# A prologue with its first x load issued ahead of the diagonal, its masks made by one sum each, and fewer filler matmuls

## The chip, the core and the metric

The kernel runs on one core of one Trainium2 chip. A core has five engines that work side by side, each through its own queue in order: TensorE (PE; PEld are its weight loads), VectorE (DVE), ScalarE (ACT), GpSimd (POOL) and SyncE (SP). SP, ACT and POOL also issue transfers, which 16 DMA engines carry out. The metric is the device time of one execution in microseconds; lower is better.

## The reference: what is computed

A causal convolution over seven tokens, with one set of seven softmax weights per head (8 heads of 24 channels), and then a multiplicative feed-forward layer:

```python
w = np.exp(weight - weight.max(-1, keepdims=True)); w = w / (w.sum(-1, keepdims=True) + 1e-9)
x_pad = np.concatenate([np.zeros((B, 6, 192)), x], axis=1)          # x: 8 x 3904 x 192
out = np.einsum('hk,bskhg->bshg', w, x_pad[:, idx].reshape(B, S, 7, 8, 24))
x = out.reshape(31232, 192)
a, b = x @ w1, x @ w2                                               # 192 x 1024 each
return (a * b @ w3) @ w_out                                         # 1024 x 1024, 1024 x 192
```

## The kernel before, in words

The 31232 tokens are cut into two streams of 15616 (four sequences each), which go through the kernel side by side, and each stream into 31 rounds of up to 512 tokens. `W_sb = w3 @ w_out` is formed once early on. A round is then a first product (`first_product`, L633: the matmuls `pa` with w1 and `pb` with w2; ScalarE copies `pa` to `asb`, L640; VectorE multiplies, L643), and a second product with `W_sb` (`second_product`, L659). 64 channels of both streams share the 128 partitions, so each weight is kept twice, as `wn` and, with its halves exchanged, as `ws` (`swap_w`, L227).

The convolution is itself a matmul. A window of 32 tokens of x (six of them before the 26 tokens that it yields) is multiplied by `Aband`, a 32x32 band matrix per head, present once in each of four groups of 32 partitions. Groups 0 and 2 hold the windows of stream 0 and 1 for the first block. Block 0 has 20 windows per stream; the first six of each are loaded by SP in float32 into `begin` (L193, L197) and cast into the block's tile `xb` (L299), the other fourteen by GpSimd with a cast on the way (`load_x(0)`, L165, one transfer per stream).

Everything that the change touches lies ahead of the first first product, in some 9 us of straight-line code. Its order is written out by hand (a manual schedule: each engine runs its instructions in the order in which the code names them, and waits are derived from the tiles). The prologue goes like this:

- `taps` is loaded, and its softmax formed: `low` (L264), the exponential on ScalarE (L265), the reciprocal (L275), and `share` (L276), which holds the weights on a diagonal over the heads.
- `diag`, a 128x136 tile with ones where the column is the partition, is made on GpSimd by a memset and `affine_select` (L200, L201). From it come `cmask` (four copies, L216) and `every` (four copies through `identities`, L270), four identities of 32x32 side by side on every group of partitions.
- TensorE spreads `share` over the partitions (`spread`, L281), VectorE copies it (`wsb`, L286) and multiplies it into the mask (`cprod`, L292), TensorE gathers that with `every` (`bps`, L305), and VectorE casts the outcome to `Aband` (L309).
- Between these TensorE runs matmuls on a tile of zeros, whose outcome nobody reads: `warm` (L246), and `fill` (L258), which has `Aband` as its operand and so stands behind it in the queue.
- GpSimd, after its two x transfers, issues eight transfers of w1 and w2 (L232 to L238), columns 0 to 384 first and 384 to 1024 second; then it swaps the first 256 columns of `wn[0]`, loads x for blocks 1 and 2, and swaps further columns.
- Then come the convolution of block 0 (`conv(0, ...)`, L345, evicted to `convo`, L355), its transposes on TensorE with a few more fillers (`first_transposes`, L435, L254, copied to `xT`, L440), the last swaps and the first product.

For stream 0 the first window begins six tokens ahead of the tensor, so its first rows in `begin` are cleared and loaded by a transfer of their own. For stream 1 one transfer loads all six windows, with six rows of the preceding sequence in the first, and these are cleared in `xb` after the cast (L301).

Of the kernel before, what the change touches and what calls it, by code (L numbers as in the profile page):

```python
# [9 lines left out]
BF16 = mybir.dt.bfloat16  # L10
AX = mybir.AxisListType
ALU = mybir.AluOpType
# [4 lines left out]
def kernel(  # L17
# [10 lines left out]
    nc = tc.nc  # L28

    B, S, D = x.shape  # L30
    H, K = weight.shape
    G = D // H
    DFF = moe_w1.shape[1]
    JT = DFF // 128
    PAD = K - 1

    NS = 2
    TS = B * S // NS
    CH = 512
# [6 lines left out]
    C = 32  # L46
    ST = C - PAD
# [7 lines left out]
    HW = 6  # L55
# [35 lines left out]
    def tok(i):  # L91
        return wins[i][0]
# [4 lines left out]
    const = ctx.enter_context(tc.tile_pool(name="const", bufs=1))  # L97
# [18 lines left out]
    x_rows = x.rearrange("b s d -> (b s) d")  # L116


    def shape_of(b):
        n = SIZES[b] // 4  # L120
        m = n // (1 if b < 3 else 2)
        return n, m, n // m

    def parts_of(b):
        return [range(4)] if 4 * shape_of(b)[1] * D <= XN else [range(2), range(2, 4)]

    xb_of, zero_rows = {}, {}

    def group(r, e):
        return slice((2 * r + e) * C, (2 * r + e) * C + C)  # L130
# [13 lines left out]
    def x_jobs(b, part):  # L144
        js = parts_of(b)[part]
        n, m, E = shape_of(b)
        tiles, zeros = xb_of.setdefault(b, {}), []

        def alloc():
            xb = work.tile([128, XN], BF16, tag="xb", bufs=5, name="xb")  # L150
            xb = xb[:, 0:len(js) * m * D].rearrange("p (w d) -> p w d", d=D)
            for j in js:
                tiles[j] = (xb, (j - js[0]) * m)
                for e in range(E):
                    for u in range(m):
                        i = FIRST[b] + j * n + u * E + e
                        if tok(i) % S == 0 and i:
                            zeros.extend(
                                (xb, group(r, e).start, tiles[j][1] + u) for r in range(NS))

        def job(first, last, r, e, s, t, w):
            def run():
                if first:
                    alloc()
                nc.gpsimd.dma_start(  # L165
                    out=tiles[js[0]][0][group(r, e), s:s + w, :],
                    in_=bass.AP(tensor=x.tensor, offset=(r * TS + t - PAD) * D,
                                ap=[[D, C], [E * ST * D, w], [1, D]]))
                if last:
                    zero_rows.setdefault(b, []).extend(zeros)  # L170
            return run

        todo = [(r, e, s, t, w) for e in range(E) for s, t, w in runs_of(b, js, e)
                for r in range(NS)]
        return [job(i == 0, i + 1 == len(todo), *a) for i, a in enumerate(todo)]

    def load_x(b):
        for part in range(len(parts_of(b))):
            for f in x_jobs(b, part):
                f()  # L180
# [4 lines left out]
    begin = work.tile([128, HW, D], FP32, tag="abT", bufs=LAG + 1, name="begin")  # L185
    zeros = const.tile([128, 128], BF16)
    nc.vector.memset(zeros, 0.0)
    for r in range(NS):
        p = group(r, 0).start
        if r == 0:  # L190
            nc.vector.memset(begin[p:p + C, 0, :], 0.0)
        w0 = 1 if r == 0 else 0
        nc.sync.dma_start(out=begin[p:p + C, w0:HW, :], in_=bass.AP(  # L193
            tensor=x.tensor, offset=(r * TS + w0 * ST - PAD) * D,
            ap=[[D, C], [ST * D, HW - w0], [1, D]]))
        if r == 0:
            nc.sync.dma_start(out=begin[p + PAD:p + C, 0, :], in_=x_rows[0:ST, :])  # L197

    diag = const.tile([128, 128 + 8], BF16)
    nc.gpsimd.memset(diag, 1.0)  # L200
    nc.gpsimd.affine_select(  # L201
        out=diag, in_=diag, pattern=[[-1, 128 + 8]], compare_op=ALU.is_equal,
        fill=0.0, base=0, channel_multiplier=1)
    ident = diag[:, 0:128]
    load_x(0)

    nc.scalar.preload_act_table(ACT.Exp)
    KP = K + K % 2
# [2 lines left out]
    share = const.tile([H, H, KP], BF16)  # L211
    nc.vector.memset(share, 0.0)
    cmask = const.tile([128, 2, C], BF16)
    for i in range(4):
        d = diag[i * C:i * C + C, i * C + 2 * i:i * C + 2 * i + C]
        nc.vector.tensor_copy(  # L216
            out=cmask[i * C:i * C + C],
            in_=bass.AP(tensor=d.tensor, offset=d.offset, ap=[d.ap[0], [1, 2], [1, C]]))

    wn = [const.tile([128, DFF], BF16, name=f"wn{k}", tag=f"wn{k}") for k in range(3)]  # L220
    wsw = [const.tile([128, DFF], BF16, name=f"ws{k}", tag=f"ws{k}") for k in range(3)]

    W0, W1, W2 = 384, 640, 768

    def swap_w(k, lo, hi, f, halves=(1, 0)):
        for h in halves:
            f(out=wsw[k][Q * h:Q * h + Q, lo:hi], in_=wn[k][Q - Q * h:2 * Q - Q * h, lo:hi])  # L227
# [3 lines left out]
    for cs in (slice(0, W0), slice(W0, DFF)):  # L231
        nc.gpsimd.dma_start(out=wn[0][:, cs], in_=moe_w1[0:128, cs])  # L232
        nc.gpsimd.dma_start(out=wn[2][0:Q, cs], in_=moe_w1[128:192, cs])
        if cs.start:
            nc.gpsimd.dma_start(out=wn[2][Q:128, cs], in_=moe_w2[128:192, cs])
        nc.gpsimd.dma_start(out=wn[1][:, cs], in_=moe_w2[0:128, cs])
        if not cs.start:
            nc.gpsimd.dma_start(out=wn[2][Q:128, cs], in_=moe_w2[128:192, cs])  # L238
# [4 lines left out]
    def warm(n, wd=CH):  # L243
        t = banks("warm")
        for j in range(n):
            nc.tensor.matmul(  # L246
                t[:, j % 2, 0:wd].rearrange("p (a c) -> p a c", c=128), zeros,
                zeros.unsqueeze(1).to_broadcast([128, wd // 128, 128]), start=True, stop=True)
        return t

    def fill(n, out, operand=None):
        for j in range(n):
            if operand is None:
                nc.tensor.matmul(  # L254
                    out.rearrange("p (a c) -> p a c", c=128), zeros,
                    zeros.unsqueeze(1).to_broadcast([128, 2, 128]), start=True, stop=True)
            else:
                nc.tensor.matmul(out, zeros, operand, start=True, stop=True)  # L258

    warm(6)  # L260

    low = const.tile([H, 1], FP32)
    total = const.tile([H, 1], FP32)
    nc.vector.reduce_max(out=low, in_=taps, axis=AX.X, negate=True)  # L264
    nc.scalar.activation(out=taps, in_=taps, func=ACT.Exp, bias=low, accum_out=total)  # L265
    every = const.tile([128, 4, C], BF16)

    def identities(i):
        ps = slice(i * C, i * C + C)
        nc.vector.tensor_copy(out=every[ps],  # L270
                              in_=diag[ps, ps].unsqueeze(1).to_broadcast([C, 4, C]))

    for i in range(3):
        identities(i)
    nc.vector.reciprocal(out=total, in_=total)  # L275
    nc.vector.scalar_tensor_tensor(  # L276
        out=share[:, :, 0:K], in0=taps.unsqueeze(1).to_broadcast([H, H, K]), scalar=total,
        in1=diag[0:H, 0:H].unsqueeze(2).to_broadcast([H, H, K]), op0=ALU.mult, op1=ALU.mult)
    spread = banks("spread")
    for i in range(4):  # L280
        nc.tensor.matmul(  # L281
            spread[i * C:i * C + C, 0, 0:2 * H].rearrange("p (h k) -> p h k", h=H),
            one_rows, share[:, :, 2 * i:2 * i + 2], start=True, stop=True)
    identities(3)
    wsb = const.tile([128, H, 2, 2], BF16)
    nc.vector.tensor_copy(  # L286
        out=wsb, in_=spread[:, 0, 0:2 * H].rearrange("p (h k) -> p h k", h=H)
            .unsqueeze(3).to_broadcast([128, H, 2, 2]))
    warm(2)

    cprod = stage.tile([128, H, 2, C], BF16, tag="cprod", bufs=1, name="cprod")
    nc.vector.tensor_tensor(  # L292
        out=cprod.rearrange("p h k (s two) -> p h k s two", two=2),
# [3 lines left out]
        op=ALU.mult)  # L297
    for r, w0, w1, f in ((0, 0, HW, A), (1, HW // 2, HW, A), (1, 0, HW // 2, V)):
        f(out=xb_of[0][0][0][group(r, 0), w0:w1, :], in_=begin[group(r, 0), w0:w1, :])  # L299
    p = group(1, 0).start  # L300
    nc.vector.memset(xb_of[0][0][0][p:p + PAD, 0, :], 0.0)  # L301
    Aband = const.tile([128, H, C], BF16)
    bps = banks("bps")
    for k in range(2):
# [3 lines left out]
            start=(k == 0), stop=(k == 1))  # L308
    nc.vector.tensor_copy(out=Aband,  # L309
                          in_=bps[:, 0, 0:C * H].rearrange("p (h s) -> p h s", s=C))  # L310
    fill(2, warm(4, 256)[:, 0, 0:2 * CH // 4], Aband.rearrange("p h s -> p (h s)"))


    xT = [const.tile([128, RING], BF16, name=f"xT{k}", tag=f"xT{k}") for k in range(NP)]
# [114 lines left out]
    def first_transposes():  # L429
        n = SIZES[0] // 4  # L430
        convo = convo_of[0]
        for k, f in enumerate((nc.scalar.copy, nc.vector.tensor_copy, nc.vector.tensor_copy)):
            tps = banks_bf16("tps")
            for w in range(n):
                nc.tensor.transpose(  # L435
                    out=tps[:, w, :],
                    in_=convo[:, w, k].rearrange("p r g -> p (r g)"), identity=ident)
            fill(min(k, 1) + 1 if k < 2 else 0,
                 tps[:, 8:16, :].rearrange("p a b -> p (a b)").bitcast(FP32)[:, 0:256])
            f(out=xT[k][:, 0:4 * n * ST].rearrange("p (c w s) -> p c w s", c=4, w=n),  # L440
              in_=tps[:, 0:n, :].rearrange("p w (c s) -> p c w s", c=4)[:, :, :, 0:ST])
# [301 lines left out]
            swap_w(k, c0, c1, P, h)  # L743

    swap_w(0, 0, 256, P)
    first_transposes()
    for k in (2, 1):
        swap_w(k, 0, W0, A, (1,))
# [25 lines left out]
    starts, chain, begun, room, p = {}, {}, set(), 0, -1  # L774
# [224 lines left out]
```

## Time and profile before

| | before |
|---|---|
| median of 3 runs | 510.67 us (510.4 to 510.77) |
| profiled execution, its own time | 510.84 us |
| span of the profiled execution | 509.1 us |
| TensorE busy in the span | 504.4 us (99%) |
| VectorE, ScalarE, GpSimd busy | 446.2, 349.6, 255.9 us |
| first matmul on zeros | at 1.07 us |
| first matmul of the convolution | at 6.52 us |
| first matmul of the first product | at 8.92 us |

The profile is one execution as the hardware profiler saw it. Rows of the timeline have start, duration, engine, line, operation, output and input, and a count; a group's start is its first instruction's. The chain of work that ended last is followed back from the end, at each step to whatever released it; in it, matmuls are counted to their modelled ends, and therefore a piece can begin a little after its instructions' own start. A transfer's time to landing is counted from its issue.

### The profile page before, as it was taken

What the parts mean: (1) busy time and instruction counts of PE and PEld (TensorE: products, weight loads), DVE (VectorE), ACT (ScalarE), POOL (GpSimd) and SP (SyncE); (2) the same over time, 40 slices, a digit from 0 to 9 for tenths busy, and PEclk for the clock granted to TensorE, in tenths of its full rate; (3) what the DMA queues carried; (4) which work ended last, traced back from release to release, by engine and by line L of the source; (5) the groups of instructions that cost most, each with busy time, mean ns of one, the idle gap of its engine ahead of it and who ended that gap; (6) DMA issues with size and microseconds to landing.
All of it is one profiled execution on the core that took longest, in us unless ns stands there. A gap on an engine that the chain in (4) does not pass through costs nothing.

```text
span 509.1 us, 13680 instructions
## 1 busy us (share of the span) xinstructions
PE 504.4 (99%) x5732; PEld 335.9 (66%) x5732; DVE 446.2 (88%) x402; ACT 349.6 (69%) x390; POOL 255.9 (50%) x340
## 2 busy tenths in 40 slices
PE   8999999999999999999999999999999999999997
PEld 4546864595569557845874596569457855965697
DVE  7898769999999799999999998999999999999930
ACT  6786667746779776577567878763876577457752
POOL 9975201332890799499879945992371056000000
PEclk9999999999999999999999999999999999999999
DMA  9999978999969769980998097629302400230025
GB/s 136 160 170 162 166 150 182 149 156 182 175 41 181 136 150 108 227 110 13 100 232 103 12 167 145 117 29 202 83 1 76 155 2 1 93 96 1 1 65 156
DMA packets 161113, 58.46 MB, mean 115 GB/s; under 512 B 116895, under 2 KB 161051, under 8 KB 161051
## 3 DMA queue, kind: packets, MB, share of 16 engines
q1 hardware_dynamic: 86107, 40.12, 37.7%
q0 software_dynamic: 74784, 17.37, 37.3%
q8 instruction: 45, 0.74, 0.6%
q14 instruction: 17, 0.14, 0.1%
q10 hardware_dynamic: 160, 0.10, 0.1%
HBM read 35.02 MB, written 34.85 MB: 137 GB/s over the span
## 4 chain that ended last, share of the span: by engine, by line
PE 99%; ACT 0%; DVE 0%; issue 0%
PE ops L659 32%; PE pa L633 31%; PE pb L633 31%; PE cps L345 1%; PE wps L731 1%; PE warm L246 1%; PE tps L420 0%; PE ops L684 0%; DVE abT L643 0%; PE tps L435 0%; PE cps L375 0%; ACT asb L640 0%; ACT convo L355 0%; PE bps L305 0%; PE warm L258 0%
## 5 line engine op out<-in xcount | busy, mean ns | idle before, releaser
L643 DVE TENSOR_TENSOR abT<-asb,pb 128x1024 bf16<-128x1024 bf16 x240 | 292.7, 1221 | 29.4 <-ACT asb L640 13.4
L640 ACT CAST asb<-pa 128x1024 bf16<-128x1024 f32 x244 | 247.0, 1012 | 64.0 <-PE pa L633 63.8
L633 PEld LDWEIGHTS <-wn 64*128 64x128 bf16 x1488 | 138.5, 94 | 82.1 <-issue 1.6
L633 PEld LDWEIGHTS <-ws 64*128 64x128 bf16 x1488 | 130.1, 94 | 70.8 <-issue 0.9
L659 PE MATMUL ops<-W_sb,abT 128*128 128x192 bf16 x1936 | 163.5, 246 | 0.0
L659 PEld LDWEIGHTS <-abT 128*128 128x128 bf16 x1936 | 158.6, 98 | 6.3 <-issue 6.3
L664 ACT COPY osb<-ops 128x768 f32<-128x768 f32 (+1 forms) x61 | 48.5, 796 | 81.8 <-PE ops L659 80.0
L633 PE MATMUL pb<-xT,wn 64*128 64x512 bf16 x376 | 103.7, 376 | 0.0
L633 PE MATMUL pa<-xT,ws 64*128 64x512 bf16 x376 | 103.5, 376 | 0.0
L633 PE MATMUL pa<-xT,wn 64*128 64x512 bf16 x376 | 103.0, 376 | 0.1
L633 PE MATMUL pb<-xT,ws 64*128 64x512 bf16 x376 | 102.2, 376 | 0.0
L633 PE MATMUL pb<-side,wn 64*128 64x512 bf16 (+1 forms) x368 | 100.4, 369 | 0.0
L633 PE MATMUL pa<-side,ws 64*128 64x512 bf16 (+1 forms) x368 | 99.4, 369 | 0.0
L633 PE MATMUL pa<-side,wn 64*128 64x512 bf16 (+1 forms) x368 | 99.4, 369 | 0.0
L633 PE MATMUL pb<-side,ws 64*128 64x512 bf16 (+1 forms) x368 | 98.1, 369 | 0.0
L538 DVE SCALAR_TENSOR_TENSOR acc<-raw,wC,acc 128x1024 f32<-128x1024 bf16 (+2 forms) x70 | 84.5, 1208 | 2.1
L596 POOL TENSOR_TENSOR acc<-acc,tmp 128x512 f32<-128x512 f32 (+6 forms) x60 | 70.4, 1177 | 4.3
L584 POOL TENSOR_TENSOR tmp<-acc,wC 128x512 f32<-128x512 bf16 x66 | 68.5, 1038 | 3.5
L920 POOL COPY pace<-abT 1x2 bf16<-1x2 bf16 x28 | 4.9, 174 | 110.0 <-DVE abT L643 110.0
L506 POOL DMA_DIRECT2D rows_c<-in_x_dram x58 | 40.7, 710 | 5.7 <-issue 2.9
L165 POOL DMA_DIRECT2D xb<-in_x_dram x50 | 31.9, 647 | 11.2 <-DMA xb<-in_x_dram 5.0
L538 DVE SCALAR_TENSOR_TENSOR acc<-side,wC,acc 128x1024 f32<-128x1024 bf16 (+1 forms) x20 | 24.4, 1218 | 3.9 <-ACT acc L520 3.4
(83 smaller groups left out, 190.6 us busy)
## 6 DMA issues: line engine op xcount, KB each, us to landing
out_dram<-osb SPq DMA_DIRECT2D x54, 384.0 KB
xb<-in_x_dram POOLq DMA_DIRECT2D x16, 240.0 KB, 7.5
out_dram<-osb SPq DMA_DIRECT2D x12, 192.0 KB
rows_c<-in_x_dram POOLq DMA_DIRECT2D x14, 130.0 KB, 6.9
rows_c<-in_x_dram POOLq DMA_DIRECT2D x14, 128.0 KB, 4.6
xb<-in_x_dram POOLq DMA_DIRECT2D x6, 228.0 KB, 7.9
w3b<-in_moe_w_dram POOLq DMA_DIRECT2D x4, 256.0 KB, 5.0
w3b<-in_moe_w_dram POOLq DMA_DIRECT2D x8, 128.0 KB, 4.3
```

The costliest lines, as they stand in the source:

```text
L165: nc.gpsimd.dma_start(out=tiles[js[0]][0][group(r, e), s:s + w, :], in_=bass.AP(tensor=x.tensor, offset=(r * TS + t - PAD) * D, ap=[[D, C] ...
L246: nc.tensor.matmul(t[:, j % 2, 0:wd].rearrange("p (a c) -> p a c", c=128), zeros, zeros.unsqueeze(1).to_broadcast([128, wd // 128, 128]), ...
L345: nc.tensor.matmul(o.rearrange("p (w g) -> p w g", g=wd)[:, :, c - c0:c1 - c0], Aband[group(r, e), h, :], xb[group(r, e), s:s + m, c:c1], ...
L506: nc.gpsimd.dma_start(out=rows_c[lo:t1, k, r * Q:r * Q + Q], in_=x_rows[r * TS + lo:r * TS + t1, k * Q:k * Q + Q])
L538: nc.vector.scalar_tensor_tensor(out=side_of[p][:, k, o:o + t1 - t0] if last else a, in0=raw[:, HALO + lo - t0 - d:HALO + hi - t0 - d], sc ...
L584: nc.gpsimd.tensor_tensor(out=acc if d == 1 else tmp, in0=pool_raw[lane][:, HALO - d:HALO - d + CH], in1=wC[:, k, K - 1 - d:K - d].to_broa ...
L596: nc.gpsimd.tensor_tensor(out=a, in0=a, in1=tmp[:, lo - t0:hi - t0], op=ALU.add)
L633: nc.tensor.matmul(p[:, r, f * N:f * N + N], w_of(i, k, r)[rs, ft * 128:(ft + 1) * 128], operand(R, k, rs), start=(k == 0), stop=(k == NP ...
L640: nc.scalar.copy(out=asb[:, :, 0:per * N], in_=pa[:, :, 0:per * N])
L643: nc.vector.tensor_tensor(out=ab[:, f0, :, 0:N], in0=asb[:, :, 0:N], in1=pb[:, :, 0:N], op=ALU.mult)
L659: nc.tensor.matmul(ops[:, g // 2, (g % 2) * D:(g % 2) * D + D], ab[:, jt, r, g * 128:(g + 1) * 128], W_sb[:, jt, :], start=(jt == 0), stop ...
L664: nc.scalar.copy(out=osb.rearrange("p (a g) d -> p a (g d)", g=2), in_=ops[:, 0:ng // 2, 0:2 * D])
```

## The change

Six edits, all in the prologue:

- `diag`'s memset moves from GpSimd to VectorE, ahead of the clears of `begin`. GpSimd issues stream 0's x transfer first, then makes the diagonal, then issues stream 1's.
- `cmask` and `every` are each made by one `tensor_reduce` over all 128 partitions, which adds up four columns of `diag`, 34 or 32 apart, instead of by four copies on 32 partitions each. `every` is now complete before the reciprocal; its fourth copy used to stand after `spread`.
- Stream 1's first window is treated as stream 0's: its rows in `begin` are cleared first, one transfer loads windows 1 to 5 and another the 26 rows of the first. The clear in `xb` goes.
- The last of the eight weight transfers, columns 384 to 1024 of `wn[1]`, moves behind the swap of `wn[0]`'s first 256 columns, ahead of x for block 1.
- The fillers: six of 512 columns become five and one of 256; two of 512 become one and one of 256; four of 256 become three; two on `Aband` become one.
- Nothing else changes: the convolution, the transposes and all that follows are the same code.

```diff
+    diag = const.tile([128, 128 + 8], BF16)
+    nc.vector.memset(diag, 1.0)
     for r in range(NS):
         p = group(r, 0).start
-        if r == 0:
-            nc.vector.memset(begin[p:p + C, 0, :], 0.0)
-        w0 = 1 if r == 0 else 0
-        nc.sync.dma_start(out=begin[p:p + C, w0:HW, :], in_=bass.AP(
-            tensor=x.tensor, offset=(r * TS + w0 * ST - PAD) * D,
-            ap=[[D, C], [ST * D, HW - w0], [1, D]]))
-        if r == 0:
-            nc.sync.dma_start(out=begin[p + PAD:p + C, 0, :], in_=x_rows[0:ST, :])
-
-    diag = const.tile([128, 128 + 8], BF16)
-    nc.gpsimd.memset(diag, 1.0)
+        nc.vector.memset(begin[p:p + C, 0, :], 0.0)
+        nc.sync.dma_start(out=begin[p:p + C, 1:HW, :], in_=bass.AP(
+            tensor=x.tensor, offset=(r * TS + ST - PAD) * D,
+            ap=[[D, C], [ST * D, HW - 1], [1, D]]))
+        nc.sync.dma_start(out=begin[p + PAD:p + C, 0, :], in_=x_rows[r * TS:r * TS + ST, :])
+
+    first_x = x_jobs(0, 0)
+    first_x[0]()
     nc.gpsimd.affine_select(
         out=diag, in_=diag, pattern=[[-1, 128 + 8]], compare_op=ALU.is_equal,
         fill=0.0, base=0, channel_multiplier=1)
     ident = diag[:, 0:128]
-    load_x(0)
+    for f in first_x[1:]:
+        f()
...
-    for i in range(4):
-        d = diag[i * C:i * C + C, i * C + 2 * i:i * C + 2 * i + C]
-        nc.vector.tensor_copy(
-            out=cmask[i * C:i * C + C],
-            in_=bass.AP(tensor=d.tensor, offset=d.offset, ap=[d.ap[0], [1, 2], [1, C]]))
+    every = const.tile([128, 4, C], BF16)
+
+    def over_groups(out, step, copies):
+        with nc.allow_low_precision("one term of the sum is 1, the others are 0"):
+            nc.vector.tensor_reduce(
+                out=out, in_=bass.AP(tensor=diag.tensor, offset=diag.offset,
+                                     ap=[diag.ap[0], copies, [1, C], [step, 4]]),
+                op=ALU.add, axis=AX.X)
+
+    over_groups(cmask, C + 2, [1, 2])
...
+        if cs.start:
+            break
         nc.gpsimd.dma_start(out=wn[1][:, cs], in_=moe_w2[0:128, cs])
...
-    warm(6)
+    warm(5)
+    warm(1, 256)
...
-    for i in range(3):
-        identities(i)
+    over_groups(every, C, [0, 4])
...
-    identities(3)
...
-    warm(2)
+    warm(1)
+    warm(1, 256)
...
-    p = group(1, 0).start
-    nc.vector.memset(xb_of[0][0][0][p:p + PAD, 0, :], 0.0)
...
-    fill(2, warm(4, 256)[:, 0, 0:2 * CH // 4], Aband.rearrange("p h s -> p (h s)"))
+    fill(1, warm(3, 256)[:, 0, 0:2 * CH // 4], Aband.rearrange("p h s -> p (h s)"))
...
     swap_w(0, 0, 256, P)
+    nc.gpsimd.dma_start(out=wn[1][:, W0:DFF], in_=moe_w2[0:128, W0:DFF])
     first_transposes()
```

More of the change, by code (lines that the diff above doesn't have):

```diff
@@ L265 @@
     nc.scalar.activation(out=taps, in_=taps, func=ACT.Exp, bias=low, accum_out=total)
[L266 to L271, printed above, removed]
-    for i in range(3):
-        identities(i)
+    over_groups(every, C, [0, 4])
     nc.vector.reciprocal(out=total, in_=total)
```

## The prediction

> **What bounds the kernel now.** I read the page first (busy time and the chain that ended last), then the chain in order of time over the first 20 us, because the change touches nothing later than that, then each engine's timeline over that stretch, and last the DMA issues with their times to landing.
>
> ```profile
> PE 99%; ACT 0%; DVE 0%; issue 0%
> ```
>
> TensorE is the bound. Windows of TensorE alone (stretch, length, busy time, instructions, granted clock, DMA share, GB/s) show where the rest lies.
>
> ```profile
> 0.00:10.00 10.00, 8.70 (x112) 1.00 0.91 131
> ...
> 505.00:509.10 4.10, 0.77 (x10) 0.89 0.61 185
> sum 509.10, PE 504.35; mean PE 50.44
> ```
>
> Of 509.10 us, 4.75 are idle: 1.30 in the first 10 us, 3.33 in the tail, which the change leaves alone, and 0.12 in all the rest. So whatever the prologue saves before the first convolution reaches the end of the kernel one for one, provided that weights and x still arrive in time. But "busy" in the prologue includes matmuls on zeros, which are there to fill time. The chain in order of time (start, duration, what) shows it:
>
> ```profile
> 1.07 2.74 PE warm L246 x6
> ...
> 4.94 0.43 PE bps L305 x2
> 5.37 0.85 PE warm L246 x4
> 6.22 0.37 PE warm L258 x2
> 6.59 0.34 PE cps L345 x16
> ...
> 13.82 0.65 PE pb L633 x6
> ```
>
> The first real work that all later work hangs on is the convolution at 6.59. The fillers stand before it in TensorE's own queue, so the chain names them. What would bind without them is read from VectorE:
>
> ```profile
> 2.38 0.15 DVE L264 TENSOR_REDUCE low<-taps 8x1 f32<-8x7 f32 x1
> 2.46 0.78 DVE L270 COPY every<-diag 32x128 bf16<-32x128 bf16 x3
> ...
> 3.45 0.27 DVE L276 SCALAR_TENSOR_TENSOR share<-taps,total,diag 8x56 bf16<-8x56 f32 x1
> ...
> 4.25 0.42 DVE L292 TENSOR_TENSOR cprod<-cmask,wsb 128x512 bf16<-128x512 bf16 x1
> 4.71 0.45 DVE L299 CAST xb<-begin 32x576 bf16<-32x576 f32 x1
> 5.23 0.14 DVE L301 MEMSET xb<- 6x96 uint32 x1
> 5.41 0.42 DVE L309 CAST Aband<-bps 128x256 bf16<-128x256 f32 x1
> ```
>
> Aband is complete at 5.41 + 0.42 = 5.83, yet the convolution starts at 6.59: 0.76 us later, all of it filler. That gap is what there is to win.
>
> **The fillers.** Removed: one half of a 512-column matmul in each of the first two groups, one 256-column matmul from the group of four, and one of the two on Aband: four times 256 columns, and 0.85 / 4 = 0.21 us each by the chain, 0.85 us in all. Not all is gained. Before the spread products, TensorE waits for share (ready 3.45 + 0.27 = 3.72) with six fillers or with five and a half; gain 0. Before bps it then waits for cprod, ready 4.25 + 0.42 = 4.67, with two fillers or with one and a half: gain 0. After bps three fillers end 0.21 earlier, at 6.01, but the single filler on Aband can't start before 5.83 plus a handover of 0.05, and that filler lasts what the first of its kind lasted (shortest, median and longest in ns):
>
> ```profile
> L258 PE MATMUL warm<-Aband,zeros x2: 367/394/421, 6.0 to 6.2; 128*128 128x256 bf16 x2
> ...
> L254 PE MATMUL tps<-zeros x3: 272/272/273, 7.9 to 8.4; 128*128 128x256 bf16 x3
> ```
>
> So the last filler ends at 5.88 + 0.42 = 6.30 instead of 6.59: **0.29 us**. That is the main term. The same rows carry a correction. A matmul of 256 columns lasts 421 ns in the first filler on Aband, 367 in the second, which ends at 6.59, and 272 among the transposes, while the windows above give a granted clock of 1.00. So TensorE became fast at about 6.5, 5.4 us after its first matmul. If that moment stays at 6.5, the first 0.2 us of an earlier convolution run at the slow rate. The cost lies between 0 and (421/272 - 1) x 0.22 (a short matmul's length; the first 16 take 0.34 together) = 0.12; I take 0.04, since most of those 16 end past 6.5. The sum is then 0.29 - 0.04 = 0.25.
>
> **GpSimd: x ahead of the diagonal.**
>
> ```profile
> 0.82 0.21 POOL L200 MEMSET diag<- 128x136 bf16 x1 [0.29 <-POOLq L983]
> 1.11 0.30 POOL L201 TENSOR_SCALAR_AFFINE_SELECT diag<-diag 128x136 bf16<-128x136 bf16 x1
> 1.54 1.48 POOL L165 DMA_DIRECT2D xb<-in_x_dram  x2
> ...
> 7.45 0.84 POOL L227 COPY ws<-wn 64x256 bf16<-64x256 bf16 x2
> ...
> 11.02 3.62 POOL L227 COPY ws<-wn 64x256 bf16<-64x256 bf16 x10
> ```
> ```profile
> xb<-in_x_dram POOLq DMA_DIRECT2D x2, 168.0 KB, 3.8
> wn<-in_moe_w_dram POOLq DMA_DIRECT2D x2, 160.0 KB, 4.7
> ```
>
> The memset of 0.21 goes to VectorE, where it costs no more than those 0.21, ahead of the mask, which can't begin before 2.0 now. Stream 0's issue (1.48 / 2 = 0.74) runs 0.82 to 1.56, the diagonal about 1.64 to 1.94 instead of 1.11 to 1.41, stream 1's issue 2.07 to 2.81, and the weights follow at 2.81, not 1.54 + 1.48 = 3.02: 0.2 earlier. With 3.8 us to landing (the last number of the two DMA rows), stream 1 lands at 5.9 instead of 2.28 + 3.8 = 6.1, stream 0 at 4.6. Both are ahead of 6.30; had the loads not moved at all, 6.1 would still be ahead of it. So the early issue gains nothing by itself, it only keeps the x out of the way of the gain. The weights' 0.2 is worth keeping, as everything that reads them moves up by 0.25.
>
> **One sum each.** The diagonal is 0.5 later, and the mask needs it. Two reductions of 256 and 512 elements per partition replace eight copies (the last one behind the share). Their price isn't in the trace. From below: the fixed 0.15 of the 8x7 reduction, plus (0.45 - 0.15) / 576 = 0.52 ns per element as in the cast of 576: 0.28 + 0.42 = 0.70. From above: share's (0.27 - 0.15) / 56 = 2.1 ns per element: 0.69 + 1.23 = 1.92. I take the Aband cast, nearest in size: (0.42 - 0.15) / 256 = 1.05 ns, so 0.42 + 0.69 = 1.11. The mask then runs 2.0 to 2.42, low 2.4 to 2.5, the identities to 3.2. The exponential waits for its table anyway:
>
> ```profile
> 1.45 1.28 ACT L207 ACT_TABLE_LOAD   x1 [1.45 <-PEq L983]
> 2.74 0.30 ACT L265 ACTIVATE taps<-taps,low 8x7 f32<-8x7 f32 x1
> ```
>
> share still starts near 3.45, so the reductions cost 0, with about 0.05 us to spare: beyond 1.16 us together they delay share, bps, Aband and the convolution one for one.
>
> **Stream 1's first rows.** The clear of 0.14 at 5.23 leaves VectorE, but Aband waited for bps there (4.94 + 0.43 = 5.37), so that gains 0. Added are a clear of begin (a few tenths at most, hidden ahead of the mask) and a fourth transfer on SP's queue:
>
> ```profile
> 1.76 0.33 SPq L193 DMA_DIRECT2D begin<-in_x_dram  x1
> ```
> ```profile
> q1 hardware_dynamic: 421, 0.29, 27.7%
> ...
> q1 hardware_dynamic: 2, 0.00, 0.1%
> ```
>
> The last two rows count the packets of SP's queue in 0 to 4 us and in 4 to 8 us: the load issued at 1.76 had all but two of its packets done by 4.0, so 2.3 us. The new one, issued behind it by 2.25, then lands at 4.55, and the cast at 4.71 needs it: hidden by 0.15, and by 0.4 before Aband is touched (the cast's 0.45 has to end by 5.41). If it took the 3.8 us of GpSimd's x it would land at 6.05.
>
> **wn[1]'s second half behind the swap.** GpSimd is through eight weight loads at 7.45 today, (7.45 - 3.02) / 8 = 0.55 each; with seven, begun 0.2 earlier, at 6.7. Then it waits for the first weights (4.7 at most after 2.81, so 7.5, where it starts today), swaps for 0.8, issues for 0.55 and comes to what is queued behind, the x of block 1 and the ten copies, 0.6 late at most. The moved weights, issued at 7.5 to 8.3, land 3.8 to 4.7 later, at 11.3 to 13.0; their copies are the third and fourth of the ten from 11.02 (0.39 each, ready at 12.6 today). So these are ready between 12.6 and 13.8. TensorE wants them for the group that the chain has at 13.82; its first matmul starts some 0.2 before that (matmuls overlap by the length of a short one), and 0.25 earlier by the change: 13.4. The middle of the bounds, 13.2, is in time, so I take 0; the worst costs 0.4.
>
> **Sum.** 0.29 - 0.04 + 0 + 0 = 0.25 us. The profiled execution took 510.84, 1.74 more than its span and 0.17 above the median; against its own time the sum is 510.59, against the median of 510.67 it is **510.4**.
>
> **The rivals.** *The fast rate comes later (slower).* With fewer fillers TensorE rests before spread, bps and the filler on Aband, for one half filler's time, 0.2 us, twice, and less the third time. If what makes it fast begins anew at a rest, 5.4 us after 3.8 is 9.2. Between the convolution and the first product lie 15 transposes and three fillers, 15 x 128 + 3 x 256 = 2688 columns, 0.21 us per 256 slow and half that fast. A slow stretch costs half its length: from about 7.3 to 9.2 that is 0.95, net 0.95 - 0.25 = +0.7, so 511.4, and 0.5 us for each further us of delay. It decides from 0.5 us of slow transposes on, where the gain is gone. For it: the rows show a rate change that the clock column doesn't. Against: each rest is shorter than one filler (2.74 / 6 = 0.46), together a tenth of the time before 6.3, and no row shows TensorE slowed by a rest. The Trainium skill ("TensorE: Matmul & The Clock Gate", Part 1: The HAM clock gate) says that the array runs at half rate until it was busy for one window of some 3.4 us, and that the windows run free of the kernel. By that rule a spoilt window means a delay of 3.4 us, to 9.9, and an estimated 511.8; a window that still counts as busy means no delay, and the sum stands. The two speeds agree with the trace; how much rest a window forgives no row shows.
>
> *The reductions are dear.* At 1.92 instead of 1.11 the chain is 0.75 late, net +0.5: 511.2. For it: they are strided and nothing of their kind is in the trace; against: of the VectorE rows above only the one of 56 elements gives such a rate.
>
> *A late arrival eats the gain.* Stream 1's first rows at 6.05 put Aband at 6.95 instead of 5.83: net +0.85, 511.5; a landing 0.25 behind 4.95, or moved weights as late as their bound, give just 510.7 to 510.8. Against: the packet counts above.
>
> *The fillers were not the limit*, and x was: then the convolution starts at 6.5 as before, 510.6. Against: the landings of 5.3 and 6.1.
>
> **How the numbers follow.** 0.2% is 1.02 us, about what a measurement of this kernel can tell from no change; the main term is a quarter of that, so most cases end within it. Chances: the forecast (510.1 to 510.6) 0.58; later fast rate 0.17, half of it above 511.7, since no row bounds the delay and some 3.3 us of it suffice; dear reductions 0.08; a late arrival 0.07, 0.01 of it above 511.7; no gain 0.04; and 0.06 for what the shifted order of transfers does in the 500 us behind, 0.03 to either side. Slower 0.085 + 0.01 + 0.03, rounded 0.13; faster 0.03; same 0.84. The range 510.0 to 511.4 leaves out the 0.06, most of the late rate and the worst arrivals, some 0.2; the forecast's own range is 510.1 to 510.6.
>
> **What would show it.** Right: stream 0's issue at 0.82 and the first weights at 2.8; the mask's reduction near 0.42 and the identities' near 0.69; share at 3.45; Aband done at 5.83; the convolution's first matmul 0.25 to 0.3 earlier, and the same shift in the first product (chain, 13.82 to about 13.6). Wrong: 256-column matmuls of 421 ns past 7 us; share later than 3.55; VectorE idle before the cast of begin; TensorE idle "<-POOL ws" or "<-DMA wn" near 13. Most likely to spoil the forecast is the moment when TensorE becomes fast.

## The result, and the profile after

The changed kernel takes 513.77 us (median of 6 runs, 512.76 to 515.56) against 510.76 (510.4 to 511.72): 3.0 us slower, a ratio of 1.006 with a 95% interval of 1.0038 to 1.0083. I had forecast 510.4, with an upper end of 511.4. Its executions also scatter over 2.8 us where those of the kernel before mostly lie within 1.

The profiled execution (513.23 us, span 511.5) is among the quicker three of them. Its chain over the first 14 us, in order of time (start, duration, what):

```profile
0.72 0.67 issue
1.39 0.82 POOL xb L165
...
2.31 0.26 POOL diag L200
2.57 4.87 DMA xb<-in_x_dram
...
7.48 0.42 PE cps L343 x11
...
8.55 0.70 PE tps L433 x5
9.25 0.21 PE tps L261
9.47 0.53 PE tps L433 x5
10.00 0.43 PE tps L261 x2
10.43 0.53 PE tps L433 x5
10.96 0.91 PE pa L631 x6
```

The kernel before had, in the same view:

```profile
7.57 0.45 PE tps L435 x5
8.02 0.11 PE tps L254
8.13 0.29 PE tps L435 x5
8.42 0.22 PE tps L254 x2
8.64 0.35 PE tps L435 x5
8.99 0.91 PE pa L633 x6
```

The first product starts at 10.96 instead of 8.99: 1.97 us later. Of that, 7.48 - 6.59 = 0.89 lies ahead of the convolution, and (10.96 - 7.48) - (8.99 - 6.59) = 1.08 behind it, where the same transposes and fillers take twice as long (0.21 a filler instead of 0.11). From there on the two executions run nearly alike: the last group of second products starts at 506.56 instead of 504.45, 2.11 later, and the remaining 0.3 of the span falls behind the last matmul, in the last outputs' transfer. That stretch differs between executions of one kernel as much: two further profiles of the changed kernel, shown below, have 5.28 and 5.05 us from that group's start to the end, this one 4.94. From block 1's convolution to the end the profiles of all kernels here take 493.1 to 494.1 us, and one 495.1, though the code is the same there. So a gain of 0.25 us in the prologue can't be read from the time of one execution.

VectorE's timeline shows the first 0.9, in part:

```profile
2.66 0.58 DVE L218 TENSOR_REDUCE cmask<-diag 128x64 bf16<-128x256 bf16 x1 [0.80 <-POOL diag L200]
3.16 0.14 DVE L272 TENSOR_REDUCE low<-taps 8x1 f32<-8x7 f32 x1
3.23 0.99 DVE L218 TENSOR_REDUCE every<-diag 128x128 bf16<-128x512 bf16 x1
...
4.32 0.27 DVE L276 SCALAR_TENSOR_TENSOR share<-taps,total,diag 8x56 bf16<-8x56 f32 x1
...
6.24 0.42 DVE L307 CAST Aband<-bps 128x256 bf16<-128x256 f32 x1 [0.22 <-PE bps L303]
```

VectorE waits 0.80 us for the diagonal, which comes at 2.63 and not at 1.94. The mask starts at 2.66 instead of 1.44, share at 4.32 instead of 3.45, and Aband is ready at 6.66 instead of 5.83. x of stream 1, issued at 2.57, takes 4.87 us to land instead of 3.8, so that the convolution begins for stream 0 at 7.02 and then stands until 7.48. TensorE's own timeline shows what the late share does to it:

```profile
4.64 0.20 PE L281 MATMUL spread<-share,one_rows 8*32 8x16 bf16 x4 [1.04 <-DVE share L276]
```

It rests for 1.04 us ahead of spread.

### The profile page after: what moved, and what is told of

The parts are those of the page before. It is cut to its first block, busy times and chain, and to the rows that moved or that the text cites. A ratio compares the mean times of both kernels' runs of the same rounds, so it can differ in the third digit from the quotient of the medians.

```text
span 511.5 us, 13673 instructions
## 1 busy us (share of the span) xinstructions
PE 505.2 (99%) x5730; PEld 335.9 (66%) x5730; DVE 446.4 (87%) x397; ACT 349.5 (68%) x390; POOL 256.0 (50%) x339
## 4 chain that ended last, share of the span: by engine, by line
PE 97%; DMA 1%; ACT 0%; DVE 0%; issue 0%; POOL 0%; POOLq 0%
PE ops L657 32%; PE pa L631 31%; PE pb L631 31%; PE cps L343 1%; PE wps L729 1%; DMA xb<-in_x_dram 1%; PE tps L418 0%; PE tps L433 0%; PE ops L682 0%; DVE abT L641 0%; PE cps L373 0%; ACT asb L638 0%; POOL xb L165 0%; PE tps L261 0%; ACT convo L353 0%
## 5 line engine op out<-in xcount | busy, mean ns | idle before, releaser
L165 POOL DMA_DIRECT2D xb<-in_x_dram x50 | 31.9, 644 | 13.2 <-DMA xb<-in_x_dram 4.8
## 6 DMA issues: line engine op xcount, KB each, us to landing
xb<-in_x_dram POOLq DMA_DIRECT2D x6, 228.0 KB, 10.3
```

Source lines behind the costliest of these rows:

```text
L165: nc.gpsimd.dma_start(out=tiles[js[0]][0][group(r, e), s:s + w, :], in_=bass.AP(tensor=x.tensor, offset=(r * TS + t - PAD) * D, ap=[[D, C] ...
```

## The experiments

Theory A: issuing x first makes the diagonal late; with it share and Aband; TensorE, with fewer fillers, rests for a microsecond, and the rest puts off the moment when its matmuls become fast. Rivals: x of stream 1 alone (theory B); the reductions; the fillers by themselves; the moved weights; the split first rows. "Ratio" is always against the kernel before on the same chip, whose median there was 510.66 to 510.82.

### Undoing parts of the change

**The diagonal first again.**

```diff
-    first_x = x_jobs(0, 0)
-    first_x[0]()
     nc.gpsimd.affine_select(out=diag, in_=diag, ...)
-    for f in first_x[1:]:
-        f()
+    load_x(0)
```

> The changed kernel with the diagonal made on GpSimd ahead of both x issues (the memset stays on VectorE); reductions and fillers as changed. Theory A: the diagonal is ready near 1.6, the reductions run from 1.6 to 3.2, share is back at 3.45 to 3.6, Aband at about 5.9; x of stream 1 is issued at about 2.4 as before the change; TensorE's rests are short, the transposes are fast, and the time is 510.4 to 511.0. Rival (reductions and fewer fillers do the harm by themselves): 512 or more.

Measured: 512.18 (511.24 to 513.02), ratio 1.0026 [1.0017, 1.0035]: 1.6 us of the 3.0 are gone. share is back at 3.41, with the reductions in place (0.53 and 0.99), and spread waits for nothing. The forecast of 510.4 to 511.0 was still too good. In this profile the matmuls stay slow until about 10.3, though TensorE rests for only some 0.3 us in all between 3.5 and 10.3, and the cast that needs stream 1's first rows waits 0.39 us for them. The chain:

```profile
8.11 0.21 PE tps L258
...
9.82 1.04 PE pa L628 x6
```

So order is the largest single part, and not the only one; and a long rest is not the only thing that goes with a late fast rate.

**Copies instead of reductions.**

```diff
-    over_groups(cmask, C + 2, [1, 2])
+    for i in range(4):
+        ...nc.vector.tensor_copy(out=cmask[i * C:i * C + C], ...)
...
-    over_groups(every, C, [0, 4])
+    for i in range(3):
+        identities(i)
...
+    identities(3)
```

> The changed kernel with the mask and the identities made by eight copies as before; all else as changed. Theory A: the reductions took 0.58 + 0.99 us, the copies' parts ahead of share about 0.91 + 0.78 with the last copy behind share; so share comes only little earlier than 4.32 (by 0 to 0.2), since the copies too begin at 2.66 when the diagonal is there. Then most of the delay of share is the diagonal's (made at 2.31 to 2.63 instead of 1.11 to 1.41) and not the reductions', and the time stays within 0.3 us of the changed kernel's. Rival (the reductions are what delays share): share near 3.5, time 512 or less.

Measured: 513.3 (512.45 to 515.01), 1.0055 [1.0039, 1.0071], no different from the changed kernel within the intervals. The copies start at 2.65 and share comes at 4.47, later than with the reductions. The reductions do not delay the chain; the diagonal does.

**The rests filled.**

```diff
-    warm(5)
-    warm(1, 256)
+    warm(8)
...
-    warm(1)
-    warm(1, 256)
+    warm(2)
...
-    fill(1, warm(3, 256)...
+    fill(3, warm(4, 256)...
```

> The changed kernel with its rests filled: eight fillers of 512 columns ahead of spread, two behind it, four of 256 after bps, three on Aband. Theory A (the late chain makes TensorE rest for 1.0 us ahead of spread, and the rest puts off the moment when its matmuls become fast, from 6.5 us to past 10): with no long rest the 256-column matmuls of the transposes last 272 ns again instead of 420, the first product starts about 1 us earlier (10.0 instead of 10.96 on the chain), and the time falls from 513.8 to about 512.8, with less scatter. Theory B (the 2 us come from the x of stream 1, which lands at 7.4, and nothing else): the transposes stay as they are and the time stays at 513.8, or grows by what the fillers take.

Measured: 512.51 (511.77 to 514.72), 1.0036 [1.0021, 1.0052]: adding some 1.9 us of matmuls on zeros (4.5 times 512 columns at the slow rate's 0.43) makes the kernel 1.3 us faster. Its matmuls are fast from 4.8 at the latest, and the first product's first matmul is at 9.32 instead of 10.89. Theory B, that x alone does it, falls. But from there to block 1's convolution it takes 8.04 us, not 6.8: GpSimd's copies of the moved weights wait 1.98 us for them, until 14.55, and TensorE for the copies.

```profile
14.55 2.72 POOL L232 COPY ws<-wn 64x256 bf16<-64x256 bf16 x8 [1.98 <-DMA wn<-in_moe_w_dram]
```

**Rests filled, and the weights back.**

```diff
-        if cs.start:
-            break
...
-    nc.gpsimd.dma_start(out=wn[1][:, W0:DFF], in_=moe_w2[0:128, W0:DFF])
```

> The changed kernel with its rests filled (eight fillers, two, four, three) and the second half of wn[1] loaded where it was before. If rests and the moved load are two separate costs: the 1.2 us between first product and block 1's convolution are gone, and the time is 511.3 to 511.6 against 512.5 with the rests filled alone; what is left above 510.8 is the late Aband (6.5 instead of 5.83) with the x of stream 1. If the moved load costs nothing: 512.5.

Measured: 512.0 (511.81 to 516.52), 1.003 [1.0006, 1.0053]. The 1.2 us are gone from the profile (6.84 between the two points), but the time falls by 0.5 only. In this execution stream 1's x landed 5.0 us after its issue and the first product started at 9.91, 0.99 later than before the change; so what remains here is the late Aband and x.

**Only the weights back.** The last diff on the changed kernel itself.

> The changed kernel with the second half of wn[1] loaded where it was before. In the profile of the changed kernel TensorE went from the first product to block 1's convolution in 6.81 us, as before the change (6.84): there the moved load was hidden by the late first product. If that holds in most executions, the time stays at 513.3 to 513.8. If many executions start their first product earlier than the profiled one, it falls by up to the 1.25 that the move costs alone: 512.5.

Measured: 514.18 (512.2 to 514.88), 1.0065 [1.0052, 1.0078]: no gain. Inside the change the moved load is hidden by the late first product, as expected. TensorE's timeline of this execution shows where the slow rate ends, within the first product:

```profile
12.46 0.63 PE L629 MATMUL pb<-xT,wn 64*128 64x512 bf16 x1
12.88 0.45 PE L629 MATMUL pb<-xT,ws 64*128 64x512 bf16 x1
12.89 0.45 PE L629 MATMUL pb<-xT,wn 64*128 64x512 bf16 x1
13.17 0.38 PE L629 MATMUL pa<-xT,wn 64*128 64x512 bf16 x1
```

A matmul of 512 columns falls from 630 to 380 ns at about 12.9. That is 2 us later than in the profile of the changed kernel (10.8), and the time is 0.8 longer, though the rows ahead of the convolution repeat within 0.1 us. In this execution the convolution does not stand for x on the chain (it begins at 7.11, not 7.48), and the first product still starts at 10.84, only 0.12 earlier: the late x of stream 1 is a small part of the loss.

**The changed kernel without order, fillers and moved weights.** Left are the reductions, the split rows and the memset on VectorE.

> The changed kernel without three of its edits: diagonal ahead of both x issues, fillers as before, the second half of wn[1] as before. Left are the reductions, the split first rows and the diagonal's memset on VectorE. If order, fillers and weights are the cause, this is at 510.8 to 511.4. If something else in the change costs, 511.8 or more.

Measured: 511.35 (511.2 to 512.52), 1.0007 [0.9985, 1.003]. So the three edits that were undone are 2.4 of the 3.0 us. As the moved weights cost nothing inside the change, that points to order and fillers; no run separates fillers from weights with the diagonal first. Of the 0.6 at the median that are left the interval can't tell whether they are real. The profile shows a part, as VectorE waits for stream 1's first rows:

```profile
5.19 0.45 DVE L292 CAST xb<-begin 32x576 bf16<-32x576 f32 x1 [0.53 <-DMA begin<-in_x_dram]
5.67 0.42 DVE L300 CAST Aband<-bps 128x256 bf16<-128x256 f32 x1
```

Aband is 0.26 later than before the change, and the first product 0.18 (9.17 on the chain); the rest of this execution's 0.7 us falls behind block 1's convolution and is not explained.

### One part alone, on the kernel before

**One long rest and nothing else.**

```diff
-    warm(6)
+    warm(4)
```

> The kernel before with four fillers of 512 columns ahead of spread instead of six, nothing else changed: TensorE rests for about 0.9 us ahead of spread, as it did for 1.04 in the changed kernel, while share, Aband, x and the weights come when they did. Theory A (a long rest puts off the moment when matmuls become fast, at a moment that differs from execution to execution): no row but the matmuls' lengths changes, some executions stay as before and others become 0.5 to 2 us slower; median 511.5 to 512.5, scatter over 2 us. Rival (the changed kernel is slow by its late Aband, x and weights alone): 510.8, scatter as before.

Measured: 511.46 (510.83 to 515.16), 1.0019 [1.0005, 1.0033]. Two fillers were taken away and nothing else, and eleven of twelve executions are above 511.2. The chain:

```profile
6.65 0.38 PE cps L345 x14
...
7.68 0.70 PE tps L435 x5
8.38 0.21 PE tps L254
...
9.79 0.97 PE pa L633 x6
```

The convolution is where it was (6.65, 6.59 before), and the first product is 0.8 us later, by slow transposes alone; the fast rate comes at about 9.3. A long rest costs by itself.

**All the change's fillers.** The three filler lines of the change.

> The kernel before with the change's fillers and nothing else of it: 5.5 + 1.5 of 512 columns, 3 of 256, 1 on Aband. This is the main term of the prediction by itself: convolution at 6.30 instead of 6.59 on the chain, 0.25 us faster (510.5). Theory A (a long rest is needed to put off the fast rate; here each rest is 0.2 us): the fast rate still comes at about 6.5 and the time is 510.5. Rival (any rest does it): 256-column matmuls of the transposes last 420 ns, and the time is 511.5 to 512.

Measured: 511.64 (510.54 to 512.62), 1.0011 [1.0002, 1.002]. The main term of my sum, run alone, is a loss. Its profiled execution (510.82) has fast matmuls from about 4.9, and its chain shows the gain that I had worked out, and more:

```profile
6.15 0.37 PE cps L347 x16
...
8.58 0.91 PE pa L635 x6
```

The convolution is 0.44 and the first product 0.41 us earlier. Even so the time is no shorter than the 510.84 of the profile before: the gain is lost again behind block 1's convolution. Eight of the eleven runs are above 511.1. That these are executions with a late fast rate is likely by the other profiles, but none of them was profiled.

**Only the two front halves.** The first two filler lines of the change.

> The kernel before with half a filler less ahead of spread and half a filler less ahead of bps, the later fillers untouched: two rests of 0.2 us, and nothing gained on the chain, as share and cprod set it. Either these rests are what made the fillers alone cost 0.85 us: then 511.3 to 511.9, with executions both near 510.7 and near 512. Or they are harmless and the cost lies behind bps: 510.8.

Measured: 510.86 (510.42 to 514.83), 1.0005 [0.9989, 1.0021]: unclear. Eight of twelve runs are below 511, four at 511.7 and above. The profiled one (512.81) is one of these. In it the matmuls become fast only at about 10.6, and the convolution also waits for x:

```profile
6.55 0.28 PE L347 MATMUL cps<-xb,Aband 32*32 32x120 bf16 x3
7.33 0.99 PE L347 MATMUL cps<-xb,Aband 32*32 32x120 bf16 x61 [0.50 <-DMA xb<-in_x_dram]
```

No transfer was touched here, and yet stream 1's x landed 4.9 us after its issue, not 3.8.

**Only the last filler.**

```diff
-    fill(2, warm(4, 256)...
+    fill(1, warm(4, 256)...
```

> The kernel before with one filler on Aband instead of two, nothing else changed: the part of the prediction's main term that brings no rest with it, since the four fillers after bps still reach 6.0 and Aband is ready at 5.83. The convolution starts 0.2 earlier at 6.3, just behind the x of stream 1 (6.2); the fast rate comes when it came. 510.6, 0.2 us faster. Rival (every filler taken out costs more than it gives): 511.0 or more.

Measured: 510.97 (510.3 to 511.21), 0.9999 [0.999, 1.0007]. No loss and no gain at the median. The profiled execution (510.36) is one of the two fastest: its matmuls are fast from about 4.0, its convolution starts at 6.16 without a wait for x, and its first product at 8.71, 0.28 earlier than before. How much of that is the missing filler and how much the early fast rate, one profile can't tell.

**Only x first.**

```diff
     diag = const.tile([128, 128 + 8], BF16)
+    first_x = x_jobs(0, 0)
+    first_x[0]()
     nc.gpsimd.memset(diag, 1.0)
     nc.gpsimd.affine_select(...)
-    load_x(0)
+    for f in first_x[1:]:
+        f()
```

> The kernel before with stream 0's x issued ahead of the memset and the diagonal on GpSimd, nothing else changed. If a first issue on GpSimd can't begin before about 1.4 whatever it waits for, as in the changed kernel (1.39 there, 0.82 predicted), it begins at 1.4 here too, the diagonal ends near 2.9, the copies move Aband from 5.83 to about 7, TensorE rests for over 1 us ahead of spread, and the time is 512 to 513. If the 1.39 came from VectorE's clears, which end at 1.21 here, the issue begins near 1.2 and everything is 0.2 earlier than that. If the predicted 0.82 holds, the diagonal ends near 2.2, Aband near 6.3, and the time is 511.3 or less.

Measured: 512.05 (511.91 to 514.65), 1.0029 [1.0014, 1.0044]. GpSimd's timeline:

```profile
1.39 0.82 POOL L165 DMA_DIRECT2D xb<-in_x_dram  x1 [0.86 <-POOLq L986]
2.21 0.23 POOL L202 MEMSET diag<- 128x136 bf16 x1
2.51 0.30 POOL L203 TENSOR_SCALAR_AFFINE_SELECT diag<-diag 128x136 bf16<-128x136 bf16 x1
2.77 0.69 POOL L165 DMA_DIRECT2D xb<-in_x_dram  x1
```

The first issue begins at 1.39 whether VectorE's clears end at 1.21 or at 1.68; they are not what it waits for. Nothing that the profile shows is. The diagonal ends at 2.81, and stream 1's x is issued at 2.77, 0.4 later than without the "early" issue. Aband is ready at 7.03. This execution shows something more. TensorE is fast early, bps at 5.93 takes 0.38 for two matmuls, and then loses the rate again. Windows of TensorE alone (stretch, length, busy, granted clock, DMA share, GB/s):

```profile
7.00:7.50 0.50, 0.42 (x14) 0.81 1.32 197
7.50:8.00 0.50, 0.50 (x52) 0.50 1.21 182
...
10.00:10.50 0.50, 0.50 (x5) 0.50 1.03 161
10.50:11.00 0.50, 0.50 (x6) 0.78 0.88 148
11.00:12.00 1.00, 1.00 (x10) 1.00 1.15 144
```

Here the granted clock itself is 0.50. With (1 - 0.81) / 0.5 x 0.5 = 0.19 us of it in the first window and (1 - 0.78) / 0.5 x 0.5 = 0.22 in the fourth, it lasts from 7.31 to 10.72, or 3.41 us. Ahead of it, between 3.9 and 7.31, TensorE had rested for 1.17 + 0.21 + 0.34 = 1.7 us.

**Only the reductions.** The diff of the copies, the other way round.

> The kernel before with the mask and the identities made by one reduction each, nothing else changed. In the changed kernel they took 0.58 and 0.99 us (predicted 0.42 and 0.69), 1.57 together against the 1.16 that the prediction allowed. From a diagonal ready at 1.41 the mask would run 1.45 to 2.0, the identities 2.1 to 3.1: in the place where the copies end at 3.24. So share stays at 3.4 to 3.5 and the time at 510.8. Rival (the reductions are dear enough to delay the chain): share at 3.9 or later, 511.3 or more.

Measured: 511.03 (510.23 to 512.48), 1.0 [0.999, 1.001]. They cost nothing where the diagonal is early:

```profile
1.44 0.58 DVE L218 TENSOR_REDUCE cmask<-diag 128x64 bf16<-128x256 bf16 x1
...
2.31 0.99 DVE L218 TENSOR_REDUCE every<-diag 128x128 bf16<-128x512 bf16 x1
3.23 0.14 DVE L272 RECIPROCAL total<-total 8x1 f32<-8x1 f32 x1
3.41 0.27 DVE L273 SCALAR_TENSOR_TENSOR share<-taps,total,diag 8x56 bf16<-8x56 f32 x1
```

**Only the split first rows.** The loop over the streams as changed, and no clear in `xb`; unlike what the expectation says, the diagonal's memset stayed on GpSimd.

> The kernel before with stream 1's first rows cleared in begin and loaded by a transfer of their own, and the diagonal's memset on VectorE ahead of them, nothing else changed. With the diagonal first, the rows landed at 4.93 and the cast that Aband stands behind began at 5.03 instead of 4.71. So Aband is 0.1 to 0.15 later, covered by the fillers' two matmuls on Aband at 6.0: 510.8 to 511.0. Rival (the transfer is the late arrival of the prediction): Aband past 6.2, 511.3 or more.

Measured: 511.42 (510.91 to 512.3), 1.0011 [1.0003, 1.002]: about 0.6 us at the median, more than expected. Its profile (512.25) doesn't show why. The two clears take 0.53 on VectorE, the mask starts at 1.64 instead of 1.44 and share 0.2 later; but the cast does not wait, Aband is ready at 5.80, and as the fast rate came early, the first product's first matmul is at 8.54, 0.38 earlier than before the change. What this execution loses, it loses later: x of a later block came 1.3 us late for its convolution, which I can't tie to the edit.

**Only the moved weights.** The weights' diff, the other way round.

> The kernel before with only the second half of wn[1] moved behind the swap of wn[0]. With the rests filled, this transfer took 6.1 us to land (issued at 8.37, landed at 14.50) and the first product stood 1.2 us before the convolution of block 1. Theory (the moved load is a cost of its own, hidden in the changed kernel by TensorE's slow matmuls): TensorE waits near 13.5 for the copies of wn[1], and the time is 511.3 to 512.0. Rival (the prediction's middle, the copies ready at 13.1): 510.8.

Measured: 512.04 (511.04 to 514.15), 1.0025 [1.0013, 1.0038]. GpSimd:

```profile
7.76 0.56 POOL L748 DMA_DIRECT2D wn<-in_moe_w_dram  x1
...
13.54 2.72 POOL L227 COPY ws<-wn 64x256 bf16<-64x256 bf16 x8 [1.59 <-DMA wn<-in_moe_w_dram]
```

Issued 0.9 later than before, the weights land 5.7 us after their issue, at 13.5, and six more copies stand behind the two that wait. From first product to block 1's convolution it takes 7.36 instead of 6.84.

### Two more profiles of the changed kernel

> The changed kernel itself, another look. If the scatter comes from the moment when matmuls become fast, the rows up to 7 us repeat within 0.1 us except for matmul lengths and x landings, and the first product starts anywhere from 9.7 to 12.5; the time follows it one for one.

> The changed kernel once more, as the look before: the same expectation, another execution.

Measured: 513.56 and 513.35. Up to 7 us their rows repeat those of the first profile within 0.03 us (share 4.32, Aband 6.24 and 6.23, x first issued at 1.39). In both the matmuls become fast inside the first product, at about 11.5, and block 1's convolution starts at 17.83 and 17.87 (17.70 in the first profile, 15.76 before the change). The expectation's range was wider than what came. No profile caught one of the slowest executions, up to 515.56, so what those do is not shown.

## Why the prediction was wrong, point by point

Two steps failed: the cost of issuing x first, which I had put at nothing and which is 1.6 of the 3.0 us, and the main term, the gain of 0.29 from the fillers, which measured as a loss.

**The fillers, 0.29 less 0.04: a gain that failed.** The step that let the last filler end at 6.30 instead of 6.59 took the fillers for waiting time. They are also part of what makes TensorE fast, and only the rival had that. Run alone, this term measured a ratio of 1.0011, not a gain; with only the last filler gone 0.9999. The steps of the sum show in one profiled execution (convolution at 6.15), with the fast rate early, and even there the time is not below 510.8. At the median they are outweighed, most likely by executions in which the fast rate comes late.

**x ahead of the diagonal: the step that failed at the greatest price.** Stream 0's issue ran 1.39 to 2.21, not 0.82 to 1.56. I read 0.82 from the memset's row and took it that a transfer could be issued at that time too. So the diagonal came at 2.63 instead of 1.94, x of stream 1 was issued at 2.57, 0.2 later than before (2.37; half of 1.48 was a poor split, as the two issues take 0.83 and 0.65), instead of 0.2 earlier, and the weights too. Everything that was to be "out of the way" got in the way: putting the diagonal first gives back 1.6 us.

**The landings.** "With 3.8 us to landing" was one sample. Over the profiles of all kernels the two x transfers took 3.5 to 5.0 us, also where nothing ahead of them was changed (4.6 with only the reductions, 4.9 with only front fillers removed). My margin of 0.4 us between landing and convolution was no margin.

**The reductions.** I took 0.42 + 0.69 = 1.11 and measured 0.58 + 0.99 = 1.57, between 1.11 and the upper bound of 1.92. The allowance of 1.16 was for a diagonal at 1.94. At 1.41 even 1.57 is hidden (ratio 1.0), and at 2.63 copies are no better (1.0055). The size was off; the harm is the late diagonal's.

**Stream 1's first rows.** Landing predicted at 4.55 and hidden by 0.15. They came at about 5.0 and 5.1 where the chain was early enough to need them (waits of 0.39 and 0.53), and the edit alone costs some 0.6 us at the median, by a way that its profile does not show. In the changed kernel they are hidden by the late chain (no wait ahead of the cast at 5.57).

**The moved weights.** The middle of my bounds had the copies ready at 13.2. Alone, the weights landed at 13.5 and their two copies were ready some 0.8 after 13.54, past the upper bound of 13.8. The bound on the landing, 4.7 us, was again taken from one execution, with other transfers around it. In the changed kernel it costs nothing (1.0065 with the weights put back).

**The rival of the late fast rate** was right in its mechanism, and its rule for the price holds: a slow stretch costs half its length, and half of 8.55 to 10.8 is 1.1, where the first profile has 1.08. Its own figures were for a stretch that begins at 7.3 (and for a delay to 9.9 its rule gives 511.7, not 511.8). It was given too little weight, since I counted rests of 0.2 us. The long rest, 1.04 us, came from the late diagonal, and I had not joined the two. On the Trainium skill's page "TensorE: Matmul & The Clock Gate" (Part 1: The HAM clock gate) a window of about 3.4 us decides the rate, and it runs free of the kernel. The 3.41 us of clock 0.50 agree with that. The scatter does not speak against it, as each group lies within 3.4 us: 10.8, 11.5, 11.5 in the changed kernel and 12.9 with the weights back, and anywhere from about 4 to 6.7 in the kernels whose fillers are whole. By the same page of the Trainium skill the rate falls after an idle window. Here the measurement differs: it fell after 3.41 us with rests of 1.7 us in them, about half of them busy.

What stays open: how much of a window may be rest. Rests of 0.2 us ahead of spread went with an early fast rate in the profiles of the filler runs (rests filled; all the change's fillers) and with a late one in two others (only the front halves, where a wait of 0.5 for x followed; the diagonal first, with rests of 0.3 in all). So a long rest is enough for a late fast rate, but the runs do not show that it is needed, nor what else decides. Nor is it settled which of the later fillers costs what when all are cut (1.0011) while the last alone is free. I did not find what GpSimd does between 0.72 and 1.39, nor what makes landings differ. No version beat the kernel before. Nor do the parts add up: alone, x first costs 1.3 us at the median, the moved weights 1.2, the fillers 0.9, the split rows 0.6 and the reductions 0.2, together 4.2, and the whole change 3.0.

## What to carry to other kernels

An instruction moved to the front of a queue moves everything behind it back by its whole duration (here an issue of 0.82 us), and a queue's first transfer issue may not start when the queue's first instruction did; look for the earliest issue that any trace shows. Matmuls on zeros ahead of a dense kernel can be part of its clock, as here, where taking two of them away cost 0.7 us at the median: shorten them only where no rest appears, and judge by many executions, because one profile shows one moment of becoming fast and one set of landings. A prologue that is tuned to a few tenths has all its margins in one place, so that small edits don't add up: here a late chain hid the moved weights, which cost 1.2 us as soon as the chain is early.

## What I had not expected of the hardware

- The granted clock column reads 1.00 from the start in most of these profiles, although matmuls of 256 columns take 421 ns there and 272 later; only in one, where the rate was first gained and then lost, does it show 0.50. The lengths of equal matmuls are the surer sign.
- A strided sum of four bfloat16 values costs 1.6 ns per input element on VectorE, (0.99 - 0.58) / 256, against 1.05 for the cast that I had taken.
- The first transfer issue on GpSimd never began before 1.39 us in any profile, and took 0.82 us where the second took 0.69 (0.83 and 0.65 with the diagonal first).
